# A gated convolution with its gradients on one core: the last turns of h between two halves, and the last forward inverse transform

## The chip, the cores and the metric

The kernel runs on one core of a Trainium2 chip. The metric is device time in microseconds (us) of one execution, and the median over the runs is given. The engines are named as in the profile: PE is TensorE (matmuls, and transposes as matmuls with an identity), DVE is VectorE, ACT is ScalarE, POOL is GpSimd, SP is SyncE. Each works through its own instructions in order and waits on the others through semaphores.

## The reference

A block with two branches is computed, and the gradients of nine of its inputs for a given output gradient. Cut to what matters:

```python
xn = layernorm(A_q)                          # 2048 x 1024
# branch A: a 4-tap shift, then a convolution over the whole sequence by FFT
kv = shift4(A_k, A_shift_k) * A_v
y  = irfft(rfft(pad(kv)) * rfft(pad(A_ssm_k)))[:2048] + kv * A_ssm_D
s  = xn * y
# branch B: a bilinear gated layer, F = 3584
h  = (xn @ B_w_gate) * (xn @ B_w_up)
g  = silu(h @ B_w_down)
out = A_q + s * g
# outputs: out and the gradients of A_q, A_k, A_v, A_shift_k, A_ssm_k, A_ssm_D,
#          B_w_gate, B_w_up, B_w_down
```

## The kernel before

The sequence of 2048 rows is cut into 16 row blocks of 128, the 3584 columns of h into 14 slabs of 256. The work on PE goes through stages: the products for h (line 645, `psg`), then `h @ B_w_down` (line 971, `psbm`) with the gates, then the gradients (lines 1327, 1344, 1422 and 1474). The convolution is written as Fourier transforms along the sequence. Part of each transform is a matmul with a table (line 235, `psF`; lines 438 and 449, `psY`), and the butterflies and the product of spectra are DVE work (`tt`, line 213, and `stt`, line 283). The forward convolution runs beside the products for h.

**A unit of h.** `gu_unit(sl, b0, 4, w, tick)` takes slab `sl` and four row blocks from `b0` on. For each of the four blocks it writes a group of eight matmuls into a PSUM tile `psg`, ACT copies it into `gut` (line 647), then `flush(5)` is called, the pending multiply `hn[0]` of the unit before is written, and `tick()` writes a stretch of the convolution. So the multiply of a unit is written after the first group of the next unit: DVE forms `hN = gate * up`, POOL's queue stores it to `Hd`, and `turn` is put on the list `later`. `flush(5)` runs a turn that has aged five calls, so a unit's turn stands some four groups behind its multiply. A turn is eight transposes on PE (line 674), one copy by ACT into `hT` (line 675) and a store by SP's queue to `HTd`. There is one PSUM tile for turns (`ps_tr`), there are two `hT` tiles and three `hN` tiles.

**The last two slabs** (12 and 13) are taken by halves of the sequence: first the row blocks 0 to 7 of both slabs, then 8 to 15. So the tiles of `XNT` that only the first half reads come free early, and weights `WD` of `B_w_down` are loaded into them (`load_wd`); the turned h of the first row blocks is loaded into `HT0` (`ht_rows`). At the start of the second half (`hf == 1`) the kernel writes the pending multiply and runs all pending turns at once: `hn[0]()`, `flush()`. After the second half `hn[0]()` is called again, and `flush()` follows behind the first matmuls of `bm_first`.

**The convolution beside it.** `conv_forward` is a generator over eight slices of 128 channels (`ds`): transforms of the filter and of the data, `product`, then the inverse. There are two forms of the inverse. `inv_dft` splits by four: `W` from a sum or difference of the halves, two butterflies into `G`, and the same again; `inv_rows` then needs eight matmuls for each pair of residues (line 449). `inv8` splits by eight: more butterflies on DVE, four of them `stt`, and `inv8_rows` needs four matmuls for each pair (line 438). `INV8` names the slices with the second form. The rows of the result, `yf`, are copied by ACT (line 749) and stored to `YFd`, which the gates load as `yf_t`.

**The order.** Each `yield` of the generator gives an estimate in us of DVE time (`net` takes off some PE time). `pump` runs the generator until the estimates it has given reach a share of `F_TOTAL`; `tick` raises that share by `cnt` over `NT`. A scheduler orders each engine's instructions; `PIN[0] = True` fixes the convolution's DVE instructions in the order in which they were written (`pinned`).

**The gates.** `gate(b, ps)` takes a finished row block of `psbm`: ACT copies it to `bm` and computes two sigmoids, DVE forms the products, POOL's queue stores them. Three PSUM tiles take turns for `psbm`.

Of the kernel before, what the change touches and what calls it, by code (L numbers as in the profile page):

```python
# [19 lines left out]
def build_kernel(  # L20
# [39 lines left out]
    def ld(out, in_):  # L60
        return nc.sync.dma_start(out=out, in_=in_)
# [25 lines left out]
    def pool(name, bufs=1, side=None, space=None):  # L87
        kw = dict(name=name, bufs=bufs, reuse_waits="tile")
        if side:
            kw["side"] = side  # L90
        if space is not None:
            kw["space"] = space
        return tc.alloc_tile_pool(**kw)
# [183 lines left out]
    FWD4_W = 8 * 2.4  # L277
# [81 lines left out]
    PROD_W = 2.3 + 4 * 2.5  # L359
# [29 lines left out]
    INV_W = 2.3 + 2.4 + 2.3 + 2.8  # L389
# [64 lines left out]
    def by_res(t, rp):  # L454

        return t.rearrange("p (c r) d -> p r c d", c=2)[:, 2 * rp:2 * rp + 2]

    def rowps(ps):
        return ps[:].rearrange("p r (c d) -> p r c d", c=2)
# [5 lines left out]
    def make_pump(gen, total):  # L465
        stt_ = {"done": 0.0, "live": True}

        def pump(frac):
            while stt_["live"] and stt_["done"] < frac * total:
                try:  # L470
                    stt_["done"] += next(gen)
                except StopIteration:
                    stt_["live"] = False

        def drain():
            n = stt_["done"]
            if stt_["live"]:
                for w in gen:
                    n += w
            stt_["live"] = False  # L480
            return n
        return pump, drain
# [127 lines left out]
    nop = lambda: None  # L610
# [7 lines left out]
    def flush(age=0):  # L618

        for e in later:  # L620
            e[0] += 1
        while later and later[0][0] >= age:
            later.pop(0)[1]()

    turn_of = [0]
    hn = [nop]
# [50 lines left out]

    h_out = []
    EIGHT = ((0, 0), (0, 1), (7, 0), (7, 1))
    INV8 = (2, 4, 6)  # L680
    SHIFT_W = 8 * 2.3

    conv_state = {"forward": True, "filters": True}
# [1 line left out]
    def conv_forward():  # L685
# [54 lines left out]
        def kvs(ds):  # L740
            return S_["kvt", ds // 2][:, :, ds % 2 * P:(ds % 2 + 1) * P]

        def tail(ds):
            G = S_.pop(("G", ds))
            yf = cs.tile([P, NB, P], BF16, name="yf")
            for rp in range(4):
                ps = (inv8_rows if ds in INV8 else inv_rows)(G, ps_y, rp)
                pe_us[0] += 0.45 if ds in INV8 else 0.9
                nc.scalar.copy(out=by_res(yf[:], rp), in_=rowps(ps))
                if rp == 3:  # L750
                    st(YFd[:, :, ds * P:(ds + 1) * P], yf[:])
                yield
# [11 lines left out]
        def half(ds, x, i, first=None):  # L764
            if (ds, int(first is not None)) not in EIGHT:
                return fwd4_half(x, i, cf, ps_cv, first)
            SP = cf.tile([P, 2, 2, 512], F32, name="SP", bufs=2)
            fwd8_half(x, i, SP, ps_cv, first, True)
            return SP
# [36 lines left out]
        for ds in range(8):  # L806
# [37 lines left out]
            def ahead():  # L844
                if ds < 7:
                    sp.append(half(ds + 1, kvs(ds + 1), len(sp)))
            yield from (inv8 if ds in INV8 else inv_dft)(KX, HX, cs, ahead if ds % 2 == 0 else None, ahead)
            if ds % 2 == 1:
                ahead()
            S_["G", ds] = HX  # L850
            tl = tail(ds)
        yield 6.0
        for _ in tl:
            yield 1.0
        cs.release()
        cx.release()
        kst.release()

    F_TOTAL = 4 * SHIFT_W + 6.0 + 8 * (0.5 + FWD4_W + 1.3 + PROD_W + INV_W) + 10.0 - 0.95 * 8 * (4 * 1.75 + 0.95 + 4 * 0.9)
    F_TOTAL += len(EIGHT) * (FWD8_W - 9.6 + 0.95 * 1.75) - 2.0  # L860
    F_TOTAL += len(INV8) * (INV8_W - INV_W + 0.95 * 1.8)
    conv = conv_forward()
    chunks = [(0, 1), (1, 1), (2, 2), (4, 4), (8, 4), (12, 4)]
    xs = [(b0, n, u8((4, 6, 7)[b0 // 4 - 1], a=4) if n == 4 else lnp.tile([P, n, D], BF16, name=f"x{b0}")[:])
# [48 lines left out]
    ps_cv = pool("ps_cv", 2, space=PSUM)  # L913
    pump, drain = make_pump(conv, F_TOTAL)
    cnt = [-5]
    NT = 24 * 8.0 + 17

    def tick(by=1):
        cnt[0] += by
        if cnt[0] == -4:  # L920
            pump((SHIFT_W + 4.05) / F_TOTAL)
        if cnt[0] >= -2:
            pump((SHIFT_W + (F_TOTAL - SHIFT_W) * (cnt[0] + 6.5) / (NT + 3.5)) / F_TOTAL)

    pump((SHIFT_W + 3.95) / F_TOTAL)
    for i_ in (4, 5):
# [10 lines left out]
    def load_wd(j):  # L937
        return ld(WD[j], B_w_down[j * 512:(j + 1) * 512, :].rearrange("(c p) d -> p c d", p=P))

    def ht_rows(bp, f0, f1):  # L940
        j = (bp % 4) * 256
        return HTd[bp // 4][f0 // 24][f0 % 24 * P:(f0 % 24 + f1 - f0) * P, j:j + 256].rearrange("(c f) s -> f c s", f=P)
# [7 lines left out]
        ld(HT0[0], ht_rows(0, 0, 16))  # L950
    for hf in range(2):
        if hf == 1:
            hn[0]()
            hn[0] = nop
            flush()
            load_wd(2)
        for sl in range(NSL - 2, NSL):
            for b0 in (8 * hf, 8 * hf + 4):
                gu_unit(sl, b0, 4, slabs[sl - NSL + 2], tick)
            if (hf, sl) == (1, NSL - 2):  # L960
                wd_ld = load_wd(3)
                ld(HT0[1][:, 8:12], ht_rows(0, 24, 28))
            if (hf, sl) == (0, NSL - 2):

                assert len(h_out) == 8
                ld(HT0[1][:, 0:8], ht_rows(0, 16, 24))
# [609 lines left out]
def kernel(  # L1576
# [22 lines left out]
    out_9: bass.AP,  # L1599
):  # L1600
    build_kernel(
        ctx, tc,
        A_q, A_k, A_v, A_shift_k, A_ssm_k, A_ssm_D, B_x, B_w_gate, B_w_up, B_w_down, grad_out,
# [32 lines left out]
```

## Time and profile before

| | |
|---|---|
| median of 3 runs | 1930.09 us (1929.29 to 1930.82) |
| the profiled execution, its own time | 1929.84 us |
| its span in the trace | 1928.1 us |
| PE busy | 1914.2 us, 99% |
| DVE busy | 1542.1 us, 80% |
| ACT busy | 638.8 us, 33% |
| POOL busy | 329.1 us, 17% |

All times inside the trace count from the start of the span; the 1.74 us between the execution's own time and the span lie around it. Two slices of the page's row per engine tell the stages apart: DVE is at 9 tenths through the products for h, falls when `psbm` begins, and is high again beside the gradients. The stages by the trace: the products for h from the start to 519 us, `psbm` to 718 us, the gradients from there on. A row of the timeline gives start, length, engine, line, operation, the tiles written and read, the count, and in brackets the idle time of the engine ahead of it and what ended it. A row of the stretches gives the stretch, its length, then for PE, PEld, DVE, ACT and POOL the busy time and the instructions, then the granted clock of PE, the share of the DMA engines and their GB/s.

### The profile page before, as it was taken

The page shows a single profiled execution, that of the slowest core. Times are in us where ns is not written, and L with a number is a line of the kernel's source. Part 1 is how long each engine was busy: PE and PEld are TensorE (multiplying, and loading weights), DVE is VectorE, ACT ScalarE, POOL GpSimd, SP SyncE. Part 2 cuts the span into 40 slices and gives each one's busy share as a digit, 9 for nine tenths or more (in the row PEclk, how much of TensorE's full clock was granted, in tenths as well). Part 3 has the DMA queues.
Part 4 walks back from the last instruction along what each step waited for, and adds up shares of the span by engine and source line. Part 5 has one row for each costly group of instructions (what it writes and reads, how often), then busy time and mean ns, then how long its engine had stood idle before and what let it go on. Part 6 is the DMA issues. An engine that isn't in the chain of part 4 may idle for free.

```text
span 1928.1 us, 27453 instructions
## 1 busy us (share of the span) xinstructions
PE 1914.2 (99%) x10978; PEld 1030.8 (53%) x10978; DVE 1542.1 (80%) x1695; ACT 638.8 (33%) x943; POOL 329.1 (17%) x461
## 2 busy tenths in 40 slices
PE   8999999999999999999999999999999999999999
PEld 5555655555444456665666666664444444444444
DVE  8999999999956555888799999999996403388884
ACT  5754655555332233343222222222222102011113
POOL 5121212201112210000122132021211101111111
PEclk9999999999999999999999999999999999999999
DMA  8776867659799988666788798585787999889984
GB/s 292 269 259 217 261 208 236 219 209 293 242 294 293 302 284 262 208 202 215 253 249 262 245 244 264 200 273 177 223 254 175 152 199 201 177 174 200 187 189 159
DMA packets 451360, 444.43 MB, mean 231 GB/s; under 512 B 268800, under 2 KB 371612, under 8 KB 436768
## 3 DMA queue, kind: packets, MB, share of 16 engines
q1 hardware_dynamic: 394848, 243.36, 47.7%
q0 software_dynamic: 40064, 169.95, 28.0%
q10 hardware_dynamic: 16320, 29.36, 4.1%
q8 instruction: 86, 1.41, 0.3%
q14 instruction: 42, 0.34, 0.1%
HBM read 194.00 MB, written 185.64 MB: 197 GB/s over the span
## 4 chain that ended last, share of the span: by engine, by line
PE 91%; DVE 6%; issue 1%; ACT 1%; DMA 0%; SPq 0%; ACTq 0%; DVEq 0%
PE psb L1344 20%; PE psx L1474 20%; PE psg L645 14%; PE psb L1327 10%; PE psbm L971 10%; PE psb L1422 9%; PE psF L235 3%; DVE W L213 2%; DVE HX L213 1%; PE tr L674 1%; PE psY L438 1%; DVE KX L213 1%; PE psY L1130 1%; PE psx L1422 1%; DVE U L213 1%
## 5 line engine op out<-in xcount | busy, mean ns | idle before, releaser
L645 PE MATMUL psg<-wslab,U 128*128 128x512 bf16 x1792 | 408.9, 380 | 3.4 <-DMA wslab<-in_B_w_gate_dram 2.5
L1344 PE MATMUL psb<-U,U 128*128 128x512 bf16 x1792 | 397.1, 379 | 0.0
L1474 PE MATMUL psx<-U,dgut 128*128 128x512 bf16 x1536 | 332.8, 379 | 0.0
L1474 PEld LDWEIGHTS <-dgut 128*128 128x128 bf16 x1792 | 175.1, 98 | 211.6
L1344 PEld LDWEIGHTS <-U 128*128 128x128 bf16 x1792 | 175.1, 98 | 198.1
L645 PEld LDWEIGHTS <-U 128*128 128x128 bf16 x1792 | 172.6, 98 | 189.0 <-issue 3.9
L1327 PE MATMUL psb<-wdt,U 128*128 128x256 bf16 x1792 | 205.6, 273 | 0.0
L1327 PEld LDWEIGHTS <-U 128*128 128x128 bf16 x1792 | 175.1, 98 | 29.4
L1422 PE MATMUL psb<-U,U 128*128 128x512 bf16 x816 | 177.1, 379 | 0.0
L213 DVE TENSOR_TENSOR W<-W 128x1024 f32<-128x1024 f32 (+1 forms) x174 | 171.5, 1002 | 3.7
L1349 ACT CAST wb<-psb 128x512 bf16<-128x512 f32 x112 | 65.6, 586 | 315.1 <-PE psb L1344 310.5
L971 PE MATMUL psbm<-U,ht 128*128 128x512 bf16 x672 | 145.7, 379 | 0.0
L1422 PEld LDWEIGHTS <-U 128*128 128x128 bf16 x896 | 87.4, 98 | 104.6
L647 ACT CAST gut<-psg 128x512 bf16<-128x512 f32 x156 | 91.4, 587 | 123.8 <-PE psg L645 123.4
L1506 ACT ACTIVATE dx_t<-dxn 128x1024 bf16<-128x1024 f32 x15 | 15.9, 1057 | 324.4 <-DVE dxn L213 324.4
L1182 DVE SCALAR_TENSOR_TENSOR dkp<-dkT,kT 128x1024 bf16<-128x1024 bf16 (+2 forms) x64 | 78.3, 1224 | 36.9 <-DMA dkT<-DKSHd 34.9
L971 PEld LDWEIGHTS <-ht 128*128 128x128 bf16 x672 | 65.5, 98 | 78.7
L213 DVE TENSOR_TENSOR U<-U,dht 128x2048 bf16<-128x2048 bf16 x56 | 68.3, 1220 | 45.7 <-ACT dht L1329 45.6
L1329 ACT CAST dht<-psb 128x512 bf16<-128x512 f32 x112 | 65.6, 587 | 116.4 <-PE psb L1327 116.4
L66 POOL DMA_DIRECT2D Hd<-hN x54 | 37.2, 688 | 296.3 <-DVE hN L213 294.1
L213 DVE TENSOR_TENSOR dxn<-psx,dxna_t 128x1024 f32<-128x1024 f32 x15 | 18.3, 1222 | 80.0 <-PE psx L1474 76.1
L1453 ACT CAST wbs<-psb 128x512 bf16<-128x512 f32 x51 | 29.9, 586 | 145.3 <-PE psb L1422 137.2
(237 smaller groups left out, 2451.5 us busy)
## 6 DMA issues: line engine op xcount, KB each, us to landing
U<-GUd SPq DMA_DIRECT2D x28, 1024.0 KB, 7.3
DGd<-U SPq DMA_DIRECT2D x28, 1024.0 KB, 6.4
GUd<-gut ACTq DMA_DIRECT2D x39, 512.0 KB, 6.1
out_dram<-wb SPq DMA_DIRECT2D x112, 128.0 KB, 4.3
U<-Hd SPq DMA_DIRECT2D x14, 1024.0 KB, 6.1
Hd<-hN POOLq DMA_DIRECT2D x54, 256.0 KB, 4.5
HTd<-hT SPq DMA_DIRECT2D x52, 256.0 KB, 3.7
ht<-HTd SPq DMA_DIRECT2D x6, 1536.0 KB, 9.7
```

The costliest lines, as they stand in the source:

```text
L213: pinned(V.tensor_tensor(o, a, b, op))
L235: mm = nc.tensor.matmul(ps[:, k].rearrange("p (c d) -> p c d", c=2), T[:, r, k, :], xr[:, r], start=(n == 0), stop=(n == len(rs) - 1 and ( ...
L645: gu_mm[0] = nc.tensor.matmul(ps[:], XNT[q][:, dc, qi * P:(qi + 1) * P], w[:, dc].rearrange("p a f -> p (a f)"), start=(dc == 0), stop=(dc ...
L647: nc.scalar.copy(out=gut[:, :, i], in_=ps[:].rearrange("p (a f) -> p a f", a=2))
L971: mm = nc.tensor.matmul(ps[:, dh * 512:(dh + 1) * 512], ht(fc)[:, i * P:(i + 1) * P], WD[fc // 4][:, fc % 4, dh * 512:(dh + 1) * 512], sta ...
L1182: ins = V.scalar_tensor_tensor(prod[:].rearrange("p r d -> p (r d)")[:, lo:H], dkT[:, 0, lo:H], 1.0, kT[:, 0, 13 + m + lo:13 + m + H], op0 ...
L1327: nc.tensor.matmul(ps[:, x * SLW:(x + 1) * SLW], DBMT[2 * hf + g][:, dc, (b % 4) * P:(b % 4 + 1) * P], wdt[:, dc, :], start=(dc == 0), sto ...
L1329: nc.scalar.copy(out=dht[:, 2 * e:2 * e + 2].rearrange("p b f -> p (b f)"), in_=ps[:])
L1344: nc.tensor.matmul(ps[:], XN[b // 4][:, b % 4, dc * P:(dc + 1) * P], dgus[b // 8][:, :, b % 8], start=(b == 0), stop=(b == NB - 1))
L1349: nc.scalar.copy(out=wb[:, dc % 2].rearrange("p a f -> p (a f)"), in_=ps[:])
L1422: nc.tensor.matmul(ps, h[:, f, b, :], DBM[b // 4][:, b % 4, dh * 512:(dh + 1) * 512], start=(b == 0), stop=(b == NB - 1))
L1474: nc.tensor.matmul(ps[:, dh * 512:(dh + 1) * 512], t[n][:, f, i * P:(i + 1) * P], WGU[n][:, f, dh * 512:(dh + 1) * 512], start=(n == 0 and ...
```

## The change

Four edits. The pending multiply and the pending turns are no longer written at once at the start of the second half; they go on with the lag that they have everywhere else. The last slice, 7, takes the inverse by eight. The convolution's last pause counts 3.0 in place of 6.0, in its total too, and the total grows by the estimate for one more slice with the inverse by eight. `NT` grows by 3.

```diff
-    INV8 = (2, 4, 6)
+    INV8 = (2, 4, 6, 7)
...
-        yield 6.0
+        yield 3.0
         for _ in tl:
             yield 1.0
...
-    F_TOTAL = 4 * SHIFT_W + 6.0 + 8 * (0.5 + FWD4_W + 1.3 + PROD_W + INV_W) + 10.0 - 0.95 * 8 * (4 * 1.75 + 0.95 + 4 * 0.9)
+    F_TOTAL = 4 * SHIFT_W + 3.0 + 8 * (0.5 + FWD4_W + 1.3 + PROD_W + INV_W) + 10.0 - 0.95 * 8 * (4 * 1.75 + 0.95 + 4 * 0.9)
     F_TOTAL += len(EIGHT) * (FWD8_W - 9.6 + 0.95 * 1.75) - 2.0
     F_TOTAL += len(INV8) * (INV8_W - INV_W + 0.95 * 1.8)
...
-    NT = 24 * 8.0 + 17
+    NT = 24 * 8.0 + 20
...
     for hf in range(2):
         if hf == 1:
-            hn[0]()
-            hn[0] = nop
-            flush()
             load_wd(2)
```

## The prediction

> **What bounds the kernel now.** I read the page's busy shares first, then the list of waits of TensorE (PE), then the timeline and the stretches around the one wait that counts, then the instruction order of both kernels on every engine. PE is busy for 1914.2 of 1928.1 us, so time can come only from its few waits, from its clock, or from instructions taken off it. This is PE's whole list of waits (columns: us in total, times, longest):
>
> ```profile
> PE tr L674 <- DVE hN L213: 3.0, 1, 3.0
> PE psg L645 <- DMA wslab<-in_B_w_gate_dram: 2.5, 2, 1.5
> PE tr L521 <- POOL ident masks.py:199: 1.4, 1, 1.4
> PE tr L597 <- DVE U L580: 1.0, 1, 1.0
> ```
>
> The other three are in the first 27 us, which the change leaves alone. The first is the flush between the halves. The timeline of PE there:
>
> ```profile
> 483.11 0.61 PE L674 MATMUL tr<-ident,hN 128*128 128x128 bf16 x8
> 483.56 1.67 PE L645 MATMUL psg<-wslab,U 128*128 128x512 bf16 x7
> 488.20 1.04 PE L674 MATMUL tr<-ident,hN 128*128 128x128 bf16 x8 [2.96 <-DVE hN L213]
> 489.02 5.04 PE L645 MATMUL psg<-wslab,U 128*128 128x512 bf16 x17
> ```
>
> Two turns stand one group of eight matmuls apart (one record of the eight is missing), and the second waits 2.96 us for a product hN. VectorE (DVE) wrote that product late, because the convolution's pinned work stood ahead of it. The stretches after it (us; the number behind the last engine is the granted clock):
>
> ```profile
> 488.10:491.50 3.40, 3.30 (x14) 1.75 (x15) 3.37 (x5) 1.50 (x2) 1.23 (x2) 0.50 1.07 410
> 491.50:495.00 3.50, 3.50 (x20) 1.77 (x19) 2.51 (x3) 1.48 (x3) 0.00 (x0) 1.00 0.99 335
> ```
>
> So PE runs at half clock for 3.4 us after the wait, and nowhere else but at the ends of the run: the granted clock of 0 to 488 us and of 491.5 to 1928 us is 1.00.
>
> **Part 1: the flush goes.** The instruction order shows that no matmul of the slabs is added or dropped. PE now runs 32 matmuls (L645), turns the one product, and turns the other two groups after that. I count from 479.66 us to the turn at 507.76 us, the next that both orders share. It is 96 matmuls, 16 transposes and 16 matmuls of psY in both. At full clock a matmul takes 0.216 us (32 in 6.91 us, from 508.21 to 515.12 us), eight transposes 0.44 us (507.76 to 508.21 us), four of psY 0.43 us (493.91 to 494.34 us). That is 20.7 + 0.9 + 1.7 = 23.3 us where the trace has 28.1, a gain of **4.8 us**. It agrees with the parts: 2.96 us of wait and half of 3.4 us of clock, 1.7, are 4.7.
>
> Does the wait come back? The moved turn reads the hN that DVE writes at 487.46 us. PE gets there after 64 matmuls, a turn and three psY: 479.7 + 13.8 + 0.4 + 1.3 = 495.2 us, 7 us after the product. The other moved turn reads an hN of 476.86 us, at 486.6 us. What is late next is settled by DVE:
>
> ```profile
> 489.38 4.63 DVE L213 TENSOR_TENSOR W<-SP 128x1024 f32<-128x1024 f32 x4
> 497.35 0.69 DVE L213 TENSOR_TENSOR hN<-gut 128x1024 bf16<-128x1024 bf16 x1 [3.34 <-ACT gut L647]
> ```
>
> DVE itself idled 3.34 us to 497.35 us, since the late PE gave it no new gut. In the new order the fourth group of that unit ends with the 48th matmul from 479.66 us, one turn and two psY among them, at 491.3 us and its copy (0.58 us) at 492.1, before DVE is free at 494.0. So DVE moves forward by 3.3 us and PE by 4.8: DVE loses 1.4 us of its lead. The last turn has hN ready at 521.75 us and PE there at 524.18: a cover of 2.4 us, which becomes 1.0. The earlier ones have more (hN at 513.83 for the turn at 522.47). I cost the moved turns at nothing.
>
> On SyncE (SP) the store of one turned tile now stands behind the 256 KB load of h that had followed it. That load waits for the other tile's store: turned at 486.6 us, copied in 1.0 us, landed 4.6 us later, about 493 us against an issue at 491.51 us now. It is first read some 40 us later, so nothing. The later SP chain (last turn, store at 525.9 us, 4.6 us to landing, then the weight load at 530.72 us with 5.6 us and the load of h at 531.15 us with 8.7 us) moves with the last turn. Had it not moved, these would land at 536.3 and 539.8 us; PE will want them at 536.0 and 539.9. So the bounds of this cost are 0 and 0.3 us, and I take 0, the chain hanging on PE itself. GpSimd's queue keeps its order.
>
> **Part 2: the last inverse transform in eight parts.** PE loses 16 matmuls of 128x256. Eight take 0.88 us now (539.08 to 539.96 us), four take 0.44, so four row pairs save **1.75 us**, and PE is the bound there. DVE pays: today's form is these rows,
>
> ```profile
> 524.05 2.29 DVE L213 TENSOR_TENSOR W<-KX 128x2048 f32<-128x2048 bf16 x1
> 526.37 2.36 DVE L213 TENSOR_TENSOR HX<-W 128x1024 bf16<-128x1024 f32 x2
> 528.77 2.29 DVE L213 TENSOR_TENSOR W<-KX 128x2048 f32<-128x2048 bf16 x1
> 531.09 2.36 DVE L213 TENSOR_TENSOR HX<-W 128x1024 bf16<-128x1024 f32 x2
> ```
>
> 9.4 us to 533.45. The new form is in the trace too, for slice 6:
>
> ```profile
> 455.29 2.28 DVE L213 TENSOR_TENSOR W<-KX 128x2048 f32<-128x2048 bf16 x1
> 457.61 2.48 DVE L213 TENSOR_TENSOR W<-W 128x1024 f32<-128x1024 f32 x2
> 460.01 2.49 DVE L213 TENSOR_TENSOR HX<-W 128x512 bf16<-128x512 f32 x4
> ...
> 463.02 2.28 DVE L213 TENSOR_TENSOR W<-KX 128x2048 f32<-128x2048 bf16 x1
> 465.34 3.81 DVE L213 TENSOR_TENSOR W<-W 128x1024 f32<-128x1024 f32 x4
> 469.18 1.29 DVE L283 SCALAR_TENSOR_TENSOR HX<-W 128x512 bf16<-128x512 f32 x2
> ...
> 471.00 1.29 DVE L283 SCALAR_TENSOR_TENSOR HX<-W 128x512 bf16<-128x512 f32 x2
> ```
>
> From 455.29 to 472.32 us, less two products hN of 0.6, that is 15.8 us: 6.4 more. DVE starts it at 524.05 - 3.3 = 520.7 and ends at **536.5 us**. PE's order has the first psY 16 matmuls later than before: 538.87 - 4.8 + 16 x 0.216 = **537.5 us**. Today's cover of 5.4 us shrinks to 1.0; what it costs if that goes is rival (a). ScalarE copies the same four tiles as before. Behind DVE's longer work nothing else waits: its next instruction came 17.5 us later and waited for ScalarE.
>
> **Part 3: the weights of the pump** (3.0 for 6.0, 20 for 17, the longer list). By the instruction order they shift nothing but those psY: no DVE, ScalarE or GpSimd instruction of the convolution changes place, apart from one pair of sigmoids of a later gate. Nothing.
>
> **Behind it.** YFd's store follows the last psY: 545.16 - 4.8 + 3.5 - 1.3 = 542.5 us, against PE's own shift of 6.5, so the first gate lags PE by some 3 us more. The PSUM tile that gate frees is wanted again a whole row block (12.1 us) after PE left the pair, and by 584 us ScalarE waits for PE again (6.41 us), so nothing reaches PE. From there to the end PE has no wait of its own, and 6.5 us pass through.
>
> **Sum:** 4.8 + 1.75 = 6.5 us off the profiled execution's 1929.84 (span 1928.1) gives 1923.3. It lay 0.25 us under the median of the runs, 1930.09, so the forecast for a median is **1923.6 us**.
>
> [...] Here 2.96 us were enough for a clock of 0.50. [...]
>
> **The rivals.** (a) DVE doesn't come forward, and the wait moves to the last turn or the first psY. For it: DVE is busy 118.3 of the 120 us from 240 to 360 us, so a backlog is plausible. Against it: its idle 3.34 us. Unmoved, it writes the last hN at 521.75 us, PE asks at 519.4: 2.3 us of wait, with the half clock behind it 4.0; psY is then met (539.9 both). 1925.9 to 1927.6 us. (b) The half clock stays though the wait goes: 6.5 - 1.7 = 4.8, 1925.3 us. (c) The change does not do what it says: the wait comes back at the moved turn, if hN is there 7 us later than in the trace; only psY's 1.75 stays, 1928.3 us. (d) **Slower:** the transform in eight runs much longer on DVE than in slice 6. It decides from DVE's end at 537.5 us; each us beyond is a us of PE, with 1.7 of clock after some 3. At 548 us the loss is 10.5 + 1.7 against 6.5: 1935.8 us. Against it: 15.8 us measured in this kernel would have to be 27.
>
> **How the numbers follow.** Forecast 76%, (a) 13%, (b) 5%, (c) 3%, (d) 3%. A measurement tells 0.2% from no change, 3.9 us: faster is below 1926.2. The forecast, (b) and the cheap half of (a) are: 76 + 5 + 6 = 87%. Same: the dear half of (a) and (c), 10%. Slower: 3%. The range goes from 1922.5 (the forecast less the runs' own spread, 1929.29 to 1930.82, and 0.3) to 1926.2, where (b) and the cheap half of (a) are in and 13% is out.
>
> **What would show it.** PE's list of waits without the L674 row; clock 1.00 from 484 to 495 us; the turn of 507.8 at 503.0 us; hN of 497.35 at 494.0; the transform in eight from 520.7 to 536.5 and no PE wait at psY; the first matmul of row tiles at L1327 6.5 us earlier than 718.3. A wait at L674 or psY after 515 us, or a half clock anywhere later, would make it wrong.

## The result and the profile after

The changed kernel takes 1923.36 us (median of 21 runs) against 1929.57 us for the kernel before (21 runs, the first three among them). The ratio is 0.9972, with a 95% interval of 0.9960 to 0.9983. The forecast was 1923.6 us. Some runs of either kernel are several us longer than the rest (1932.56 us for the changed one); no profile here shows why, and the medians count them.

The profiled execution has a span of 1920.8 us, 7.3 under the one of before. 0.84 us of this was gained ahead of the flush: the last turn before it begins at 477.50 us, where it began at 478.34. Of that, 0.80 us is there at the first product of h (9.09 us for 9.89), which the change doesn't touch. So 0.84 is added below wherever a time after is set against a forecast or a time before.

The longest of PE's waits in the changed kernel (us in total, times, longest):

```profile
PE psg L645 <- DMA wslab<-in_B_w_gate_dram: 2.4, 2, 1.3
PE tr L521 <- POOL ident masks.py:199: 1.4, 1, 1.4
PE tr L597 <- DVE U L580: 0.8, 1, 0.8
PE tr L606 <- DVE U L580: 0.7, 1, 0.7
```

The row for L674 is gone. Four more rows, of 0.6 us and three times 0.2, end the list. Two of them, for copies by ACT that `psF` needs, are new, at 0.2 us each; all the rest belongs to the first 41 us. The stretch of the old wait and of the half clock:

```profile
484.00:495.00 11.00, 10.95 (x69) 6.07 (x69) 10.87 (x14) 5.79 (x10) 1.90 (x3) 1.00 0.98 329
```

PE is busy for 10.95 of 11 us at a granted clock of 1.00. The timeline of PE, first at the two moved turns and then at the last inverse:

```profile
485.73 0.61 PE L674 MATMUL tr<-ident,hN 128*128 128x128 bf16 x8
...
494.42 0.61 PE L674 MATMUL tr<-ident,hN 128*128 128x128 bf16 x8
...
502.21 0.61 PE L674 MATMUL tr<-ident,hN 128*128 128x128 bf16 x8
...
519.07 18.08 PE L968 MATMUL psbm<-U,U 128*128 128x512 bf16 x82
536.98 0.60 PE L438 MATMUL psY<-HX,TI 128*128 128x256 bf16 x4
537.42 1.89 PE L968 MATMUL psbm<-U,U 128*128 128x512 bf16 x7
```

The shared turn, at 507.76 us before, stands at 502.21, or 503.05 with the start's shift: 4.7 us earlier. The first psY needs 0.44 us for its four. DVE's side:

```profile
493.15 0.68 DVE L213 TENSOR_TENSOR hN<-gut 128x1024 bf16<-128x1024 bf16 x1
...
519.86 2.29 DVE L213 TENSOR_TENSOR W<-KX 128x2048 f32<-128x2048 bf16 x1
...
533.29 2.50 DVE L283 SCALAR_TENSOR_TENSOR HX<-W 128x512 bf16<-128x512 f32 x4
```

There is no idle time in brackets ahead of the hN any more, and the inverse by eight ends at 535.79 us, 1.2 us ahead of its reader on PE. The first matmul of the gradients (line 1327, now 1324) is at 711.01 us for 718.31: 7.3 us, and 6.5 without the start's shift.

### The profile page after: what moved, and what is told of

The parts are those of the page before. It is cut to its first block, busy times and chain, and to the rows that moved or that the text cites. A ratio compares the mean times of both kernels' runs of the same rounds, so it can differ in the third digit from the quotient of the medians.

```text
span 1920.8 us, 27294 instructions
## 1 busy us (share of the span) xinstructions
PE 1902.7 (99%) x10828; PEld 1028.9 (54%) x10962; DVE 1548.5 (81%) x1705; ACT 638.9 (33%) x943; POOL 328.7 (17%) x461
## 4 chain that ended last, share of the span: by engine, by line
PE 82%; DVE 7%; issue 4%; DMA 4%; ACT 2%; SPq 0%; POOL 0%; DVEq 0%; ACTq 0%; POOLq 0%
PE psb L1341 20%; PE psg L645 19%; PE psb L1324 10%; PE psbm L968 10%; PE psb L1419 9%; PE psx L1471 6%; PE psF L235 3%; DVE dkp L1179 2%; DMA dkT<-DKSHd 1%; PE tr L674 1%; DVE dxn L213 1%; PE psY L438 1%; PE psY L1127 1%; DMA dkh<-DKSHd 1%; PE psx L1419 1%
## 5 line engine op out<-in xcount | busy, mean ns | idle before, releaser
L645 PE MATMUL psg<-wslab,U 128*128 128x512 bf16 x1734 | 401.7, 379 | 6.1 <-DMA wslab<-in_B_w_gate_dram 2.4
L213 DVE TENSOR_TENSOR W<-W 128x1024 f32<-128x1024 f32 (+1 forms) x180 | 177.7, 1004 | 3.9
```

Of the source, the lines that this page charges most:

```text
L213: pinned(V.tensor_tensor(o, a, b, op))
L645: gu_mm[0] = nc.tensor.matmul(ps[:], XNT[q][:, dc, qi * P:(qi + 1) * P], w[:, dc].rearrange("p a f -> p (a f)"), start=(dc == 0), stop=(dc ...
```

## The experiments

**The flush alone (e1).** The last hunk of the diff and nothing else.

```diff
-            hn[0]()
-            hn[0] = nop
-            flush()
             load_wd(2)
```

> The kernel before with the flush between the halves taken out and nothing else. Theory (the flush cost PE its wait and the half clock behind it): the L674 wait of 3.0 us is gone, the clock stays at 1.00 from 484 to 495 us, and the time is 4.8 us under before, a ratio of 0.9975. Rival (the half clock has another cause and stays): 3 us, 0.9985. Rival (DVE does not come forward and the wait goes to the last turn at 524 us): 0.8 to 2.5 us, 0.9987 to 0.9996.

Measured: 1924.46 us, ratio 0.9979 (0.9971 to 0.9988), 4.1 us. The wait is gone and the clock of the profiled execution is 1.00 up to the end. By the medians it is 4.6 us, against 1929.02 us for 35 runs of before beside it. The first theory holds; its 4.8 us are a little more than was measured, for the reason that the next run shows.

**The inverse by eight alone (e2).** The list and the weights, with the flush kept.

```diff
-    INV8 = (2, 4, 6)
+    INV8 = (2, 4, 6, 7)
...
-        yield 6.0
+        yield 3.0
... (the 6.0 in F_TOTAL becomes 3.0 too)
-    NT = 24 * 8.0 + 17
+    NT = 24 * 8.0 + 20
```

> The kernel before with the last slice's inverse by eight and the three weights of the pump, the flush kept. Theory (16 matmuls less on PE, DVE's longer work covered): the 3 us wait and the half clock as before; psY without a wait, its four at 0.44 us each; 1.75 us under before, a ratio of 0.9991. DVE ends the inverse at about 540 us and PE reaches the first psY at 542.3, a cover of 2.4. Rival (DVE's 6.4 us reach PE): a wait at psY of 1 us or more, and a ratio of 0.9996 to 1.000.

Measured: 1927.07 us, ratio 0.9991 (0.9983 to 1.0000). DVE ends the inverse at 537.27 us, PE begins psY at 539.81 with no wait, and the four take 0.44 us. That is the 1.75 us by the ratio, though its interval reaches 1.0000; the split by clock below puts it at 1.7 us. With e1 it adds up to 5.8 us against 5.4 for both (ratio 0.9972). What was not expected is the clock. The timeline of PE in its profiled execution, and the stretch behind the wait:

```profile
487.06 0.62 PE L674 MATMUL tr<-ident,hN 128*128 128x128 bf16 x8 [3.00 <-DVE hN L213]
487.51 3.83 PE L645 MATMUL psg<-wslab,U 128*128 128x512 bf16 x17
```

```profile
488.00:491.50 3.50, 3.50 (x19) 1.71 (x18) 3.46 (x4) 1.92 (x4) 0.56 (x1) 1.00 1.06 416
```

The wait is the same 3.00 us, and the 17 matmuls behind it take 3.83 us, not 5.04: the clock did not fall this time. Each run also lists its mean granted clock, and 3.4 us at one half take 0.0009 off a mean over the whole run. Of 35 runs of the kernel before, made beside these experiments, 11 have 1.000 (median 1927.44 us), 21 have 0.999 (median 1929.21) and 3 have 0.998. Of 23 more, beside e5 to e7, 9 have 1.000. So the half clock follows this wait in about two runs of three, and costs 1.8 us where it does. In e2 5 of 12 runs have 1.000 (median 1925.77 us, 1.7 under before's 1927.44) and 6 have 0.999 (1927.55, 1.7 under 1929.21). In e1 10 of 11 have 1.000 (1924.37 us): 3.1 us under before's 1927.44, the wait alone, and 4.8 under 1929.21, the wait and the clock.

**The wait filled (e4).** The kernel before, with 13 matmuls on PE in place of the wait.

```diff
+            if fill[0]:
+                fps = ps_y.tile([P, 512], F32, name="psY")
+                for _ in range(fill[0]):
+                    mm = nc.tensor.matmul(fps[:], ident[:], XNT[3][:, 0:4, 0:P], start=True, stop=True)
+                fill[0] = 0
+                with tc.issue_after(mm.ins):
+                    flush()
             flush(5)
...
             hn[0]()
             hn[0] = nop
-            flush()
+            later.pop(0)[1]()
+            fill[0] = 13
             load_wd(2)
```

> The kernel before with 13 matmuls of 128x512 (2.8 us, their result is thrown away) put on PE where it waits for the flush's second product; nothing else changes. It tells the clock's share from the wait's. Theory (the half clock comes from PE standing idle 2.96 us): the wait shrinks to about 0.2 us, the clock is 1.00 through 484 to 495 us, and the time falls by the clock's share alone, 1.7 us, a ratio of 0.9991, though no product comes earlier. Rival (the half clock has another cause, at that place or time): clock of 0.50 for 3.4 us near 488 us as before, ratio 1.000.

Measured: 1927.42 us, ratio 0.9991 (0.9983 to 1.0000), and all 11 runs at a clock of 1.000. The place in PE's timeline:

```profile
484.47 2.97 PE L652 MATMUL psY<-U,ident 128*128 128x512 bf16 x13
487.45 0.62 PE L682 MATMUL tr<-ident,hN 128*128 128x128 bf16 x8
487.90 3.62 PE L646 MATMUL psg<-wslab,U 128*128 128x512 bf16 x15
```

No product comes earlier, PE does 2.8 us of useless work, and the median falls to that of the runs of before whose clock stayed up (1927.44). The ratio's interval reaches 1.0000, so the time alone would not show it; the clock does, with 11 of 11 runs at 1.000 against 11 of 35. So the clock's fall at this place is due to PE standing idle, and rival (b) is refuted.

**Without the weights (e3).** The changed kernel with `yield 6.0`, the 6.0 in the total and `NT` of 17 put back.

```diff
-        yield 3.0
+        yield 6.0
... (the 3.0 in F_TOTAL becomes 6.0 too)
-    NT = 24 * 8.0 + 20
+    NT = 24 * 8.0 + 17
```

> The changed kernel with the three weights of the pump left as before (6.0, 6.0 and 17). The list of slices with the inverse by eight raises the pump's total, so the convolution is written earlier against the ticks: by the instruction order the turns, the hN products and the psF matmuls stand elsewhere in the whole stage of psg. The prediction took the weights to shift nothing but the last psY; that holds only for the three together with the list. Theory A (the weights put the stage's order back, and without them PE meets late DVE work again): one or more waits of PE at L674 or psY of 1 to 4 us in the stage, 1 to 8 us over the changed kernel, a ratio to before of 0.998 to 1.002. Theory B (the order moves but the covers hold): the time of the changed kernel, 0.997.

Measured: 1928.57 us, ratio 0.9997 (0.9989 to 1.0006), 5.2 us over the changed kernel. The first rows of its list of PE's waits:

```profile
PE tr L674 <- DVE hN L213: 1.8, 1, 1.8
PE psF L235 <- DVE kv L213: 1.7, 1, 1.7
PE psF L235 <- ACT SP L257: 1.6, 2, 0.9
```

These are 5.1 us. Theory A holds: the estimate of one more inverse by eight raises the total, every share of it that a tick asks for becomes more work, the convolution is written earlier against the groups, and PE meets late work in four places: two products of DVE and two copies by ACT. Which of the weights it is was not told apart. Only the first wait is where the expectation put it (the last turn, at 524.31 us); the second is at 409.81 us, at the shift's product. None of the four, 1.8 us at most, brought a half clock in the profiled execution, and 10 of 11 runs have 1.000.

**A longer inverse (e5, e6).** The changed kernel with the first sum of the last inverse computed once or twice more.

```diff
+        for _ in range(more):
+            tt(W[:, 0:8, :], Y[:, 0:8, :], Y[:, 8:16, :], ADD)
         tt(W[:, 0:8, :], Y[:, 0:8, :], Y[:, 8:16, :], ADD)
```

> The changed kernel with the first sum of the last slice's inverse computed twice (one DVE instruction of 2.3 us more, the same result). In the changed kernel DVE ends that inverse at 535.8 us and PE reaches the first psY at 537.0: a cover of 1.2 us. Theory (the cover is what the timeline shows): PE waits 1.1 us at psY, the clock stays at 1.00 in all runs, and the time is 1.1 us over the changed kernel, about 1924.5, a ratio to before of 0.9978. Rival (any wait of PE late in the stage brings the half clock): 2.8 us over, 0.9987. Rival (the real cover is longer, since psY reads only its own rows of the result): no wait, 0.9972.

Measured: 1922.93 us, ratio 0.9970 (0.9958 to 0.9982), no wait at psY in PE's list. DVE ends at 538.23 us, 1.2 us after PE began psY at 537.06; the first four psY take 0.89 us for 0.60. The rival on the rows is right: of the last four DVE instructions the first pair of residues reads the results of the first and the third, not of the last, and only its last matmul needs the third. So the true cover was about 2 us, the 2.3 us added less the 0.3 us that the four took longer, and not 1.2.

> The same with two such instructions, 4.6 us more: this is rival (d) of the prediction at a small size, its price and its threshold. Theory: PE waits 3.4 us at psY, and in some two thirds of the runs or more the mean clock is 0.999 (half clock for 3.4 us, 1.7 us lost), as after the 3.0 us wait of the kernel before; the runs at clock 1.000 lie 3.4 us over the changed kernel (1926.7), those at 0.999 lie 5.1 over (1928.4); ratio to before 0.999 to 0.9995. Rival (the clock does not follow waits): all runs at 1.000 and 1926.7.

Measured: 1926.68 us, ratio 0.9989 (0.9980 to 0.9997). The timeline of PE:

```profile
536.99 0.38 PE L440 MATMUL psY<-HX,TI 128*128 128x256 bf16 x2
538.73 0.27 PE L440 MATMUL psY<-HX,TI 128*128 128x256 bf16 x1 [1.36 <-DVE HX L283]
539.94 0.27 PE L440 MATMUL psY<-HX,TI 128*128 128x256 bf16 x1 [0.94 <-DVE HX L283]
```

Two waits, 2.3 us in all. In 6 of 11 runs the clock is 1.000, five of them between 1925.08 and 1925.98 us, the middle one, 1925.15, 2.2 over e5's median; in 5 it is 0.999, four of them at 1926.7 to 1926.9. So the clock does follow waits, though the median is the rival's 1926.7, and it does in nearly half of the runs (5 of 11) of a kernel whose profiled execution, at 1.00, shows only 1.36 and 0.94 us with a single matmul between them. The theory's wait of 3.4 us and its two thirds of the runs were both too much, by the cover that e5 found. The price of rival (d) was right in kind. Its threshold, DVE's end at 537.5 us, was some 1 us too early, and the 5 runs at 0.999 came with 2.3 us of wait in the profiled execution, not "after some 3".

**One more slice, two more slices (e7).** The changed kernel with slice 5, and then 3 and 5, by eight as well.

```diff
-    INV8 = (2, 4, 6, 7)
+    INV8 = (2, 4, 5, 6, 7)
...
-    NT = 24 * 8.0 + 20
+    NT = 24 * 8.0 + 23
```

> The changed kernel with slice 5 by eight too, and NT 3 more again. PE loses 16 matmuls, 1.75 us; DVE gains 6.4 us in a stage where it is busy 99%. Theory A (DVE is the second bound there, its covers are 1 to 2.4 us): PE meets waits worth more than 1.75 us, the time is 0 to 5 us over the changed kernel, ratio to before 0.997 to 1.000. Theory B (the work is put off behind the stage, where DVE has 10 us free): 1.75 us under the changed kernel, 0.9963.

> The same with slices 3 and 5, NT 7 more than in the changed kernel. Theory A: more waits, the time is 2 to 10 us over the changed kernel, ratio to before 0.998 to 1.002. Theory B: 3.5 us under the changed kernel, 0.9954.

Measured: with 5, 1925.66 us, ratio 0.9985 (0.9975 to 0.9996), 2.3 us over the changed kernel; with 3 and 5 (and `NT` of 27), 1941.97 us, ratio 1.0068 (1.0048 to 1.0087). Theory A holds for slice 5: past the start PE waits 1.9 us for a copy by ACT into `gut`, 1.4 us for two copies that `psF` needs and 0.8 us at psY, against the 1.75 us that are saved. For two slices its direction holds and its size does not: 18.6 us over the changed kernel, where 2 to 10 were expected. PE's longest waits with slices 3 and 5:

```profile
PE psg L645 <- ACT gut L647: 8.5, 3, 5.8
PE tr L1232 <- DVE dbm L213: 2.7, 1, 2.7
PE psY L438 <- DVE HX L283: 2.4, 1, 2.4
```

The mean clocks of its six runs are 0.995 to 0.998, so half clocks are in that loss too. The largest waits are for copies by ACT, and ACT itself was held up. In its order, the copy of a turn into `hT` stands ahead of the copy that PE waits for, and it began at 475.36 us after 5.62 us of waiting for the store of an earlier turned tile by SP's queue. With slice 5 alone the same wait of ACT is 3.65 us. So a queue that the prediction had watched only in passing is the one that gives way; why that store lands late stays open. The same execution shows the clock after waits of several lengths. Four rows of PE's timeline, and four stretches:

```profile
469.30 3.61 PE L645 MATMUL psg<-wslab,U 128*128 128x512 bf16 x15 [2.04 <-ACT gut L647]
478.74 3.57 PE L645 MATMUL psg<-wslab,U 128*128 128x512 bf16 x8 [5.83 <-ACT gut L647]
553.06 0.27 PE L438 MATMUL psY<-HX,TI 128*128 128x256 bf16 x1 [2.39 <-DVE HX L283]
722.45 0.62 PE L1232 MATMUL tr<-ident,dbm 128*128 128x128 bf16 x8 [2.67 <-DVE dbm L213]
```

```profile
467.00:475.60 8.60, 3.82 (x18) 1.64 (x17) 8.53 (x10) 1.32 (x3) 0.67 (x1) 1.00 1.00 316
475.70:482.40 6.70, 3.66 (x10) 1.36 (x10) 3.33 (x4) 3.53 (x6) 0.67 (x1) 0.50 0.76 239
554.20:557.50 3.30, 3.02 (x10) 1.55 (x11) 0.61 (x2) 0.85 (x2) 0.00 (x0) 0.50 0.00 0
557.60:1900.00 1342.40, 1335.50 (x7362) 714.71 (x7430) 1014.54 (x1139) 325.45 (x497) 220.56 (x302) 1.00 0.85 229
```

The half clock came with the waits of 5.83 and 2.39 us; with those of 2.04 and 2.67 us the clock stayed at 1.00.

No run beats the changed kernel: e5's 1922.93 us beside 1923.36 lies within the spread of the runs, and e5 only computes more.

## Why the prediction was right

**Part 1, the flush.** Right in place and mechanism, point by point: no wait at either moved turn, the shared turn at 503.05 us against 503.0 forecast, the hN of DVE's old idle time at 493.99 against 494.0. The prediction's list of PE's waits was not whole: three rows of 0.7, 0.6 and 0.2 us were left out, all in the first 41 us, so nothing rests on them. Nor is the clock lower at the ends of the run: it is 1.00 in the first 12 and the last 18 us. The term that was mis-sized is the clock's. The prediction took 1.7 us as certain because the one profiled execution showed it; 24 of 35 runs have it (a clock of 0.999 or 0.998), so it is worth about 1.2 us on the mean, and the flush about 4.2 in place of 4.8. e1 measured 4.1 by its ratio. A median lies in the larger group, and there the 4.8 us are right, which is why the forecast time came out all the same. Some of its closeness is luck: the three runs that it starts from have a median 0.5 us above that of the 21.

**Part 2, the inverse by eight.** Right: 1.75 us on PE (e2: 0.9991), and DVE from 520.70 to 536.63 us against 520.7 to 536.5. The first psY is at 537.82 us against 537.5. The cover of 1.0 us was the distance from DVE's end to PE's first psY, and that was too strict: e5 and e6 show about 2 us.

**Part 3, the weights.** "Nothing" was right of the weights and the longer list together. It doesn't mean that either does nothing: the instruction orders showed no shift because the two cancel. e3 shows what the weights hold off: 5.2 us, nearly all of the gain.

**Behind it.** Right. The last psY is at 542.58 us against 542.5, the next stage starts 6.5 us earlier, and PE has no wait from there on.

**The rivals.** (a) did not happen: DVE came forward by 3.4 us. (b) is refuted by e1 and e4: without the wait the clock stays up. (c) did not happen. (d) was tried in small by e6.

A wait of 2.96 to 3.0 us brought a mean clock below 1.000 in two runs of three (38 of 58 of the kernel before), and e6's waits of 2.3 us together one in 5 of 11. The same wait does not always do it: in e2's profiled execution the clock stayed at 1.00 after 3.00 us. No run shows what decides it.

## What to carry to other kernels

Where PE is busy 99%, look for the one wait left in the middle of its list, and then ask what the same order costs the engine that was late: here DVE had idled 3.3 us because PE was late in turn, so both moved forward. An estimate that paces one engine's work against another's is part of an edit: after adding work to it, compare the orders with and without the corrected weights, since the edit alone can lose all that it gains. Price the clock's fall after a wait as a chance, from the mean clocks of many runs (here below 1.000 in 38 of 58, after a wait of 2.96 us in the profile), and not from one profile.

## What the runs showed of the hardware

In these runs a half clock after an idle PE came in some executions and not in others. By the mean clock of each run (below 1.000), after 2.96 to 3.0 us of wait it came in 24 of 35 and 14 of 23 runs of the kernel before and in 7 of 12 of e2; after 1.36 and 0.94 us with one matmul between (e6) in 5 of 11; with the wait filled (e4) in none of 11. In 5 of 21 runs of the changed kernel and 1 of 11 of e1 the mean clock is below 1.000 as well, though their profiles show no such wait; those runs are 3.7 us or more longer than the median of their kernel's runs at 1.000, and none of them was profiled.

In the kernel before, the clock falls at 488.06 us and rises at 491.47, 3.41 us later. With slices 3 and 5 by eight it is at 0.50 from 475.70 to 482.40 us, for 6.7 us, and from 554.20 to 557.50 us, for 3.3 us. A fall need not begin as PE takes up work: in the kernel before it came 0.14 us ahead of the turn at 488.20 us that ended the wait, and with slices 3 and 5 between 475.60 and 475.70 us, 2.7 us into the wait of 5.83 us.

Nor does the length of a wait alone decide it: in the execution with slices 3 and 5 the half clock came with a wait of 2.39 us and not with one of 2.67 us, and after 3.00 us in e2's profiled execution the clock stayed at 1.00. What decides it was not shown. In 1 run of 11 in e3 and 4 of 12 with slice 5 the mean clock is below 1.000 as well, where the longest waits of the one profiled execution past the start are 1.8 and 1.9 us; how long PE waited in the other runs isn't recorded.
